# Two-level products in the second half of unit 7, with GpSimd making their sums

## The chip, the cores and the metric

The kernel runs on one core of one Trainium2 chip. Its engines work through queues of their own: TensorE (PE; PEld are its weight loads), VectorE (DVE), ScalarE (ACT), GpSimd (POOL) and SyncE (SP), which issues nearly all DMAs. The metric is the device time of one execution in microseconds; a kernel is given by the median of its runs.

## The reference

A pooled attention is followed by a two-layer network with a snake activation. All of it is f32.

```python
def _attn_ref(q, k, v):                      # (8, 8, 576, 64) each
    k_p = k.reshape(B, H, Sp, pool, D).mean(axis=3)     # pool = 8
    v_p = v.reshape(B, H, Sp, pool, D).mean(axis=3)
    scores = scale * np.matmul(q, k_p.transpose(0, 1, 3, 2))
    scores = scores - np.max(scores, axis=-1, keepdims=True)
    attn = np.exp(scores)
    attn = attn / (np.sum(attn, axis=-1, keepdims=True) + 1e-09)
    return np.matmul(attn, v_p)

def _moe_ref(x, w_in, w_out, alpha):         # x: 4608 x 512, w_in: 512 x 2048
    h = x @ w_in
    s = np.sin(alpha * h)
    g = h + s * s / (alpha + 1e-09)
    return g @ w_out                         # w_out: 2048 x 512
```

The attention's output, its heads side by side, is x.

## The kernel before

**Stages.** The 4608 tokens are cut into nine units of 512 (u = 0 to 8), and the 2048 hidden columns into four groups (J = 0 to 3, n = 4u + J). While the first layer runs for unit u, the attention of batch u + 1 is computed beside it, so that x of unit u + 1 is ready in time; units 7 and 8 have no attention beside them. The activated values g go through HBM (`g_bridge`, method `store_g`, action `st`), and from about 509 us on the second layer runs (`outputs`, line 1309), which reads them back.

**A group.** Its matrix product is done by a Strassen-Winograd scheme: seven products p = 1 to 7 of sums of blocks. The sums of w_in's blocks are made once (tiles a.. and as..), those of x for every unit: `sums_of_x` (line 985; items sx0 to sx3, and sn0 to sn3 for units 1 and 8) writes four blocks into the tile `bt`. A product has four matmuls, M*p*.0 to M*p*.3, each of 128 weights columns by 256 moving columns (`product` in `group`, line 1031). The partial results lie in four PSUM banks, b1, b6, b5, b7, and are carried from bank to bank by copies: c16, c67 (ACT, line 1002), p5 to an SBUF tile. Then a00, a01, a11 add on DVE (line 1001), s.. are sines and q.. squares on ACT (lines 1108 and 1115), f10 adds on DVE and f1 on POOL (line 1060), and st stores the h tile, in two DMAs, one for each half. The h tiles have two buffers, so a group's first write (a00 or a later addition) comes after the store of the group two before it.

**Two-level products.** Some products are themselves done by seven smaller ones of 128 x 128 x 128 (`inner_products`, line 1117; the table `INNER`, line 41): in units 1 to 6, p = 1 in every group and p = 5 in groups 0, 2 and 3, and in group 2 (`INNER_J`) also p = 6 and 7. The steps are i.a, i.b, i.d, i.e1, i.e5 on PE (j.a and so on for the pair 6, 7), each matmul 128 columns wide (line 1130). Between them ACT copies partial results inside PSUM (ca, line 1143; cb, line 1150) and to a small tile (cm, line 1147), and DVE adds (ad, line 1153). The operands of the small products need sums of their own: those of w_in are made once in unit 0 (`inner_w_in`, `inner_w_more`), those of x in every unit by POOL (`inner_x`, `inner_y`, line 983). A group with the pair 6, 7 is begun with a copy of b1 to the tile `seed` (c1); its p5, c16 and c67 are additions on DVE, it has an addition a10 on DVE, and its f10 is on POOL.

**Order.** Every step is an item with a key: 28 to a unit, 7 to a group, plus the number in the table `ORDER`. `perform` (line 1098) issues the items in order of their keys, and this alone sets the order in every engine's queue. The table has a row for the attention's items of a middle unit (`U`), and one for each kind of group (`kind`, line 1087): `first0` to `first3`, `enter`, `mid0` to `mid3`, `exit` (the last group of unit 6), and `end0` to `end3` for both units 7 and 8. `U7` holds sn0 to sn3 and `R` the second layer's preparation: from unit 7 on `load_w_out` (line 837) copies w_out's blocks into place on ACT (line 861) and makes their sums on DVE (line 870), in the steps w0 to w10, and `inner_w` (line 883) follows in v1 to v5, with the tiles we1 and we2 for p = 1 and 2.

**Room.** x of unit u lies in the tile `home` u mod 3; home 0 held unit 6 and isn't used after it. The pool `wo`, with we1 and we2, is opened when unit 7 begins.

```python
        two = self.two(u)
        G.l2 = tuple(p for p in INNER if two and J in INNER[p] and n > self.NJ)
        ...
        G.more = (6, 7) if two and J in INNER_J else ()
        ...
    def two(self, u):
        return 0 < u < self.B - 1
```

Of the kernel before, what the change touches and what calls it, by code (L numbers as in the profile page):

```python
# [13 lines left out]
F32 = mybir.dt.float32  # L14
# [27 lines left out]
INNER_J = (2,)  # L42
ORDER = {
# [5 lines left out]
    "pool_vm": 14.29103999, "pool_v": 15.39643495, "pool_k1": 19.10087875, "clean": 19.11669555, "move": 19.31117787, "values": 24.09941715,  # L49
    "out4": 24.12754471, "qb": 24.20188937, "qc": 24.32802831, "qa": 24.3322157, "out0": 24.34194636, "out2": 24.34888708, "out3": 24.38197436,  # L50
    "k_t": 24.38256879, "sx0": 24.38397247, "qd": 24.39556784, "k_c": 24.4069381, "inner_x": 24.72116763, "out1": 25.02433978, "mark": 25.50536264,
    "sx1": 25.50540264, "qe": 25.61120273, "sx2": 25.78068113, "sx3": 31.53281643},
# [147 lines left out]
class Kernel:  # L200
# [752 lines left out]
    def inner_y(self):  # L953
# [10 lines left out]
        self.sums([(t4[k], R(1, 0)[:, k], t2[:, k], OP.subtract) for k in range(2)])  # L964
        for k, p in enumerate((6, 7)):
            self.X2[p] = {1: R(0, 0)[:, k], 2: R(1, 0)[:, k], 3: R(1, 1)[:, k], 4: t4[k], 5: t1[k], 6: t2[:, k], 7: t3[:, k]}

    def inner_x(self, u):

        steps = []  # L970
# [666 lines left out]
```

## Time and profile before

| | us |
|---|---|
| median of 3 runs (901.91 to 905.1) | 901.98 |
| the profiled execution | 900.14 |
| its span, first to last instruction | 898.4 |
| PE busy | 890.7 |
| DVE busy | 654.3 |
| ACT busy | 456.4 |
| POOL busy | 313.6 |

The profiled execution's own time is 1.7 us above its span and 1.84 us below the median. In the rows quoted below, times are microseconds from the span's start. A row of the timeline gives start, length, engine, line, operation, written and read tiles, the shape, how many instructions were merged, and in brackets the idle time before and what ended it. A row of groups gives the count, the busy time, the mean in nanoseconds and the idle time before. A row of waits gives who waited for whom, the sum, how often, and the longest. An f32 matmul stands in the trace as two records.

### The profile page before, as it was taken

The page shows a single profiled execution, that of the slowest core. Times are in us where ns is not written, and L with a number is a line of the kernel's source. Part 1 is how long each engine was busy: PE and PEld are TensorE (multiplying, and loading weights), DVE is VectorE, ACT ScalarE, POOL GpSimd, SP SyncE. Part 2 cuts the span into 40 slices and gives each one's busy share as a digit, 9 for nine tenths or more (in the row PEclk, how much of TensorE's full clock was granted, in tenths as well). Part 3 has the DMA queues.
Part 4 walks back from the last instruction along what each step waited for, and adds up shares of the span by engine and source line. Part 5 has one row for each costly group of instructions (what it writes and reads, how often), then busy time and mean ns, then how long its engine had stood idle before and what let it go on. Part 6 is the DMA issues. An engine that isn't in the chain of part 4 may idle for free.

```text
span 898.4 us, 18664 instructions
## 1 busy us (share of the span) xinstructions
PE 890.7 (99%) x7218; PEld 816.5 (91%) x7218; DVE 654.3 (73%) x1004; ACT 456.4 (51%) x1079; POOL 313.6 (35%) x327
## 2 busy tenths in 40 slices
PE   8999999999999999999999999999999999999997
PEld 5887888979889898888888999999999999999997
DVE  7575767667566675754346999979798888889894
ACT  5686877878877887877876611111111111121111
POOL 4899967666677766462221200000000000000000
PEclk9999999999999999999999999999999999999999
DMA  9966858667695765557226346251618172534401
GB/s 254 225 199 159 250 173 235 163 187 191 190 266 142 206 196 150 159 161 272 93 101 209 131 129 185 80 182 41 215 39 226 28 220 46 173 92 142 123 14 41
DMA packets 128753, 141.19 MB, mean 157 GB/s; under 512 B 46920, under 2 KB 95704, under 8 KB 128664
## 3 DMA queue, kind: packets, MB, share of 16 engines
q1 hardware_dynamic: 125880, 137.88, 52.9%
q10 hardware_dynamic: 2784, 2.11, 0.9%
q8 instruction: 57, 0.93, 0.4%
q14 instruction: 32, 0.26, 0.1%
HBM read 75.37 MB, written 47.19 MB: 136 GB/s over the span
## 4 chain that ended last, share of the span: by engine, by line
PE 98%; DMA 0%; DVE 0%; ACT 0%; issue 0%; ACTq 0%; DVEq 0%
PE PS L1359 43%; PE PS L1031 39%; PE PS L1130 9%; PE PS L464 2%; PE PS L761 2%; PE PS L774 1%; DMA q<-in_q_dram 0%; PE PS L575 0%; PE PS L554 0%; PE PS L1195 0%; PE PS L421 0%; PE PS L435 0%; PE PS L719 0%; PE PS L362 0%; PE PS L717 0%; PE PS L629 0%
## 5 line engine op out<-in xcount | busy, mean ns | idle before, releaser
L1031 PE MATMUL PS<-home,a 128*128 128x256 f32 x920 | 234.6, 381 | 0.0
L1031 PEld LDWEIGHTS PS<-home,a 128*128 128x128 f32 x920 | 169.6, 190 | 25.6 <-issue 4.7
L1031 PE MATMUL PS<-home,as 128*128 128x256 f32 x680 | 182.3, 382 | 0.0
L1031 PEld LDWEIGHTS PS<-home,as 128*128 128x128 f32 x680 | 123.5, 190 | 14.9 <-POOL as L833 0.2
L1409 POOL TENSOR_TENSOR cc<-cc,cb 128x576 f32<-128x576 f32 x1 | 2.0, 1982 | 373.5 <-DVE cb L1314 373.5
L1060 POOL TENSOR_TENSOR h<-h,s 128x1024 f32<-128x1024 f32 x36 | 86.0, 2390 | 111.6 <-ACT s L1115 109.0
L1359 PE MATMUL PS<-s,wb 128*128 128x144 f32 x896 | 119.1, 286 | 0.0
L1359 PEld LDWEIGHTS PS<-s,wb 128*128 128x128 f32 x896 | 113.6, 190 | 0.0
L1115 ACT ACTIVATE s<-s,c 128x256 f32<-128x256 f32 (+1 forms) x216 | 112.6, 580 | 0.0
L1495 ACT COPY PS<-PS 128x144 f32<-128x144 f32 x56 | 14.7, 263 | 144.1 <-PE PS L1359 138.6
L1108 ACT ACTIVATE s<-h,al 128x256 f32<-128x256 f32 x156 | 69.9, 503 | 21.0 <-DVE h L1001 11.4
L1001 DVE TENSOR_TENSOR h<-PS,s 128x512 f32<-128x512 f32 x66 | 44.4, 684 | 47.3 <-ACT s L1115 35.3
L1359 PE MATMUL PS<-r,wb 128*128 128x144 f32 x512 | 73.3, 286 | 0.0
L1359 PE MATMUL PS<-s,a 128*128 128x144 f32 x512 | 73.2, 286 | 0.0
L1001 DVE TENSOR_TENSOR h<-PS,p 128x512 f32<-128x512 f32 x72 | 48.9, 686 | 27.4 <-PE PS L1031 20.5
L1359 PEld LDWEIGHTS PS<-r,wb 128*128 128x128 f32 x512 | 67.1, 190 | 0.1
L1359 PEld LDWEIGHTS PS<-s,a 128*128 128x128 f32 x512 | 67.0, 190 | 0.0
L290 POOL TENSOR_TENSOR kvin<-kvin 96x768 f32<-96x768 f32 (+3 forms) x42 | 65.0, 1548 | 4.9 <-DMA a<-in_moe_w_in_dram 1.6
L1108 ACT ACTIVATE s<-PS,al 128x256 f32<-128x256 f32 x132 | 55.5, 475 | 10.3 <-PE PS L1031 9.5
L1477 ACT COPY PS<-PS 128x144 f32<-128x144 f32 x56 | 14.7, 263 | 88.3 <-PE PS L1359 88.3
L1359 PE MATMUL PS<-x,wb 128*128 128x144 f32 x384 | 54.9, 286 | 0.0
L1359 PE MATMUL PS<-s,we 128*128 128x144 f32 x384 | 54.7, 286 | 0.0
(239 smaller groups left out, 1609.3 us busy)
## 6 DMA issues: line engine op xcount, KB each, us to landing
g_bridge<-h SPq DMA_DIRECT2D x72, 512.0 KB
r<-g_bridge SPq DMA_DIRECT2D x31, 1152.0 KB
out_dram<-o SPq DMA_DIRECT2D x122, 72.0 KB
kvin<-in_k_dram SPq DMA_DIRECT2D x14, 576.0 KB
q<-in_q_dram SPq DMA_DIRECT2D x7, 1024.0 KB
kvin<-in_v_dram SPq DMA_DIRECT2D x14, 512.0 KB
ex<-tr SPq DMA_DIRECT2D x54, 92.0 KB
ex<-tr SPq DMA_DIRECT2D x54, 88.0 KB
```

The costliest lines, as they stand in the source:

```text
L290: self.nc.gpsimd.tensor_tensor(out=t[..., 0:w] if w > D else out, in0=t[..., 0:w], in1=t[..., w:2 * w], op=OP.add)
L464: nc.tensor.matmul(ps[e][r0 + r:r0 + r + q.shape[-1], h, :], q[s], kb[s, hp, :], start=(e, r0 + r) not in begun, stop=True, skip_group_che ...
L761: nc.tensor.matmul(o[r:r + 64], w, x, start=start and i < 2, stop=False, skip_group_check=True)
L1001: add = lambda o, x, y: nc.vector.tensor_tensor(out=o, in0=x, in1=y, op=OP.add)
L1031: nc.tensor.matmul(ps[:, jj, :], self.A[p][:, kk, f * P:(f + 1) * P], x[:, kk, :], start=start and p not in G.begun, stop=(kk == 1), skip_ ...
L1060: "f1": lambda: nc.gpsimd.tensor_tensor(out=g()[:, :, :, 1], in0=g()[:, :, :, 1], in1=G.s()[:, :, :, 1], op=OP.add),
L1108: self.nc.scalar.activation(out=G.s()[:, i, jj, j, :], in_=src[:, jj], func=AF.Sin, scale=self.al[:, f:f + 1])
L1115: self.nc.scalar.activation(out=x, in_=x, func=AF.Square, scale=self.c[:, f:f + 1])
L1130: nc.tensor.matmul(out, W[m][:, G.J - (INNER_J[0] if p > 5 else 0)], self.X2[p][m], start=start, stop=True, skip_group_check=True)
L1359: nc.tensor.matmul(out, W[:, J // 2, J % 2, :], A[:, J, :], start=(start and J == 0), stop=(J == self.NJ - 1), skip_group_check=True)
L1477: nc.scalar.copy(out=st["x1"][:, 1, :], in_=st["x1"][:, 0, :])
L1495: nc.scalar.copy(out=x1[:, 0, :], in_=x0[:, 1, :])
```

## The change

Unit 7's groups 2 and 3 take two-level products: p = 1, 5, 6, 7 in group 2 and p = 1, 5 in group 3 (`late`, `LATE_J`). Their weights' sums can't be those of unit 0, whose tiles are gone with the attention's pools, so POOL makes them again: `late_w` makes 16 for group 2 and 8 for group 3, in we1 and we2, which lend their room before `inner_w` needs it; the 8 for group 3 overwrite those of p = 1 and 5 of group 2. `late_x` makes the 16 sums of x in home 0. The tiles `seed` and `m5` of unit 7 lie in we2 also. `W2_at` notes from which group on a product's small weights count.

Unit 7's groups 1 to 3 have rows of their own in `ORDER` (`late1` to `late3`), U7 has the new items, and the rows `U`, `end0`, `end1`, `exit`, `mid1` and `mid3` have new numbers; the other rows stay.

```diff
 INNER_J = (2,)
+LATE_J = (2,)
...
 "U7": {
-    "sn0": 27.5, "sn2": 27.50625, "sn1": 27.51, "sn3": 28.24964},
+    "late_x0": 0.9616694, "late_w20": 6.12700667, "late_x1": 6.13293975, "late_w21": 6.13376164, "late_w30": 16.10735295, "sn0": 23.28925745,
+    "sn1": 24.89864805, "sn2": 26.09347972, "sn3": 29.05819944},
...
+    def late_x(self, ps):
+
+        u, bt = self.B - 1, self.bt
+        if 1 in ps:
+            self.room = self.home(0, [P, self.K1, 2 * TH])[:].rearrange("p a b -> p (a b)").rearrange("p (n i m) -> p n i m", i=4, m=P)
+        for p in ps:
+            x = self.xT[u][:, 0:2, 0:TH] if p == 1 else bt[:, p - 5]
+            R = lambda i, j: x[:, i, j * P:(j + 1) * P]
+            t1, t2, t3, t4 = (self.room[:, (1, 5, 6, 7).index(p), i] for i in range(4))
+            self.sums(((t1, R(0, 1), R(0, 0), OP.subtract), (t2, R(1, 1), t1, OP.subtract), (t3, R(1, 1), R(0, 1), OP.subtract), (t4, R(1, 0), t2, OP.subtract)))
+            self.X2[p] = {1: R(0, 0), 2: R(1, 0), 3: R(1, 1), 4: t4, 5: t1, 6: t2, 7: t3}
+
+    def late_w(self, J, ps):
+
+        if J == 2 and 1 in ps:
+            a, b = (self.wo.tile([P, 3, 2, 2, P], F32, name=f"we{i}")[:].rearrange("p a b c d -> p (a b c) d") for i in (1, 2))
+            self.late = [a[:, i:i + 1] for i in range(12)] + [b[:, i:i + 1] for i in range(4)]
+            self.seed = b[:, 4:8].rearrange("p (j i) d -> p j (i d)", j=JW)
+            self.m5 = b[:, 8:10].unsqueeze(2)
+        for p in ps:
+            n = (1, 5, 6, 7).index(p)
+            s1, s2, s3, s4 = self.late[4 * n:4 * n + 4]
+            A = self.A[p][:].rearrange("p k (J j m) -> p k J j m", j=2, m=P)
+            L = lambda i, j: A[:, j, J:J + 1, i]
+            self.sums(((s1, L(1, 0), L(1, 1), OP.add), (s2, s1, L(0, 0), OP.subtract), (s3, L(0, 0), L(1, 0), OP.subtract), (s4, L(0, 1), s2, OP.subtract)))
+            self.W2[p] = {1: L(0, 0), 2: L(0, 1), 3: s4, 4: L(1, 1), 5: s1, 6: s2, 7: s3}
+            self.W2_at[p] = J
...
-        G.l2 = tuple(p for p in INNER if two and J in INNER[p] and n > self.NJ)
+        late = u == self.B - 1 and J > 1
+        G.l2 = tuple(p for p in INNER if late or two and J in INNER[p] and n > self.NJ)
...
-        G.more = (6, 7) if two and J in INNER_J else ()
+        G.more = (6, 7) if late and J in LATE_J or two and J in INNER_J else ()
...
+        if J and u == self.B - 1:
+            return f"late{J}"
...
+        if u == last:
+            for i, ps in enumerate(((1, 5), (6, 7))):
+                at(ORDER["U7"][f"late_x{i}"], self.late_x, ps)
+                for J in LATE_J if i else range(2, self.NJ):
+                    at(ORDER["U7"][f"late_w{J}{i}"], self.late_w, J, ps)
```

Of the new numbers, those that move an item past items of another step (the key is the group's 7n or the unit's 28u plus the number; `mid3` numbers above 7 fall into the next unit):

```diff
 U:    inner_y  8.278 -> 11.712   move 19.311 -> 17.136   sx1 25.505 -> 26.733   sx2 25.781 -> 27.574   inner_x 24.721 -> 25.026
 mid3: q1 12.624 -> 14.114   s01 6.362 -> 14.644   q01 8.176 -> 15.264   f1 16.353 -> 18.660   f10 18.569 -> 18.809   st 18.713 -> 18.943
 exit: f10 10.100 -> 13.134   st 10.168 -> 13.799
```

In a middle unit's keys, f10 of the group before stood at 11.569, ahead of shift3 (11.586), norm0 (11.956) and a01, i.ad and a11 of groups 0 and 1; it now stands at 11.809, behind them and behind norm0 (11.803).

Group 2's steps on PE in unit 7, in the new order, between the last matmul of unit 6 and its own: 38 matmuls of groups 0 and 1, i.a, nine matmuls of group 1, i.b, j.a, i.d, two matmuls, j.b, i.e1, two matmuls, j.d, four matmuls of group 2, j.e6, i.e5, j.e7; then group 3's i.a, three matmuls, i.b.

More of the change, by code (lines that the diff above doesn't have):

```diff
@@ L42 @@
 INNER_J = (2,)
+LATE_J = (2,)
 ORDER = {
 "U": {
[4 rows of a table removed]
[L49 to L52, printed above, removed]
[4 rows of a table added]
+    "pool_vm": 13.97674974, "move": 17.13639355, "pool_v": 18.90634272, "pool_k1": 21.55942806, "clean": 23.9684371, "values": 24.09941715,
+    "qa": 24.23841769, "qc": 24.2794839, "qb": 24.39685794, "out4": 24.42836383, "out0": 25.02338312, "out2": 25.02339305, "out3": 25.02339681,
+    "sx0": 25.02340266, "k_t": 25.02341133, "qd": 25.0263071, "k_c": 25.02636605, "inner_x": 25.02638612, "out1": 25.05042092, "mark": 25.06929668,
+    "qe": 25.5242967, "sx1": 26.73277002, "sx2": 27.57350582, "sx3": 31.42990609},
 "F": {
@@ L938, in inner_w_in @@
         self.W2[p] = {1: L(0, 0), 2: L(0, 1), 3: s4, 4: L(1, 1), 5: s1, 6: s2, 7: s3}
+        self.W2_at[p] = 0
     def inner_w_more(self):
@@ L951, in inner_w_more @@
             self.W2[p] = {1: L(0, 0), 2: L(0, 1), 3: s4, 4: L(1, 1), 5: s1, 6: s2, 7: s3}
+            self.W2_at[p] = n[0]
     def inner_y(self):
@@ L1129, in product @@
             W = self.W2[p]
-            nc.tensor.matmul(out, W[m][:, G.J - (INNER_J[0] if p > 5 else 0)], self.X2[p][m], start=start, stop=True, skip_group_check=True)
+            nc.tensor.matmul(out, W[m][:, G.J - self.W2_at[p]], self.X2[p][m], start=start, stop=True, skip_group_check=True)
         def products(*ms):
@@ L1145, in cm @@
         def cm():
-            m5.append(self.sm.tile([P, 2, 1, P], F32, name="m5", bufs=1)[:, 0:k])
+            m5.append((self.m5 if G.u == self.B - 1 else self.sm.tile([P, 2, 1, P], F32, name="m5", bufs=1))[:, 0:k])
             nc.scalar.copy(out=m5[0], in_=y[:, :, 1:2])
@@ L1564, in run @@
                 self.turn = 4
-                self.W2, self.X2 = {}, {}
+                self.W2, self.X2, self.W2_at = {}, {}, {}
                 self.R = {}
@@ L1575, in run @@
                 att.close()
-                wo = pool(top, "wo", 1, side="right")
+                wo = self.wo = pool(top, "wo", 1, side="right")
                 self.gp = pool(top, "gp", 1, side="right")
```

9 lines of the change are left out of this document (6 added, 3 removed), and 93 rows, old and new, of the table ORDER.

## The prediction

> **What bounds the kernel now.** I read the page first (parts 1, 2 and 4), then the chain of waits in order of time, the stretches by unit, and PE's waits.
>
> ```profile
> span 898.4 us, 18664 instructions
> PE 890.7 (99%) x7218; PEld 816.5 (91%) x7218; DVE 654.3 (73%) x1004; ACT 456.4 (51%) x1079; POOL 313.6 (35%) x327
> PEclk9999999999999999999999999999999999999999
> PE 98%; DMA 0%; DVE 0%; ACT 0%; issue 0%; ACTq 0%; DVEq 0%
> ```
> ```profile
> 407.48 101.64 PE PS L1031 x470
> 509.12 384.31 PE PS L1359 x3136
> ```
> ```profile
> 252.50:307.00 54.50, 54.50 (x487) 47.25 (x490) 36.21 (x64) 43.05 (x98) 36.76 (x42) 1.00 0.70 196
> 407.40:455.00 47.60, 47.60 (x225) 41.91 (x222) 20.38 (x28) 38.01 (x87) 10.17 (x6) 1.00 0.49 177
> ```
> ```profile
> PE PS L1195 <- DVE full L1528: 1.1, 1, 1.1
> ...
> PEld PS L1130 <- DVE PS L1153: 2.3, 6, 0.4
> ```
>
> TensorE is the path: 98% of the chain is PE, its clock is whole, and from 407.48 to the end the chain is two stretches of PE alone. Of the stretches I asked for, 252.5 to 307.0 is one middle unit and 407.4 to 455.0 is about unit 7; in both PE is busy throughout (columns: length, then PE, PEld, DVE, ACT, POOL busy, clock, DMA share, GB/s). PE's longest wait for another engine is 1.1 us, at the start. In the middle only its weight loads are held, 0.4 us at most, once per unit, behind the addition of line 1153. So the time can change in two ways only: by the work that PE is given, and by waits that PE does not have today. In unit 7 POOL is busy 10.17 of 47.60 us, ACT 38.01.
>
> **The change part by part: PE's work.** One product of one level is four matmuls of 256 columns, one of two levels is seven of 128. An f32 matmul leaves two records. Their pace is read from starts:
>
> ```profile
> 411.40 2.75 PE L1031 MATMUL PS<-home,a 128*128 128x256 f32 x12
> 413.99 3.19 PE L1031 MATMUL PS<-home,as 128*128 128x256 f32 x14
> 417.01 2.75 PE L1031 MATMUL PS<-home,a 128*128 128x256 f32 x12
> ```
> ```profile
> 301.96 0.39 PE L1130 MATMUL PS<-last,q 128*128 128x128 f32 x2
> ...
> 302.85 0.60 PE L1031 MATMUL PS<-home,as 128*128 128x256 f32 x2
> ```
>
> (417.01 - 411.40) / 26 = 0.2158 us for a record of 256 columns, and (302.85 - 301.96) / 8 = 0.1113 for one of 128 (four rows of two lie between those starts). A product then goes from 8 x 0.2158 = 1.726 to 14 x 0.1113 = 1.558 us: 0.168 saved. Group 2 of unit 7 changes four products (1, 5, 6, 7), group 3 two (1, 5): 6 x 0.168 = **1.0 us**. That is the whole gain on PE; nothing else leaves its queue.
>
> The Trainium skill, "TensorE: Matmul & The Clock Gate", section "Wait — 56ns, not 53.3ns?", has a warm matmul take its columns at 2.4 GHz and a fixed 2.5 ns; if a record is two passes that would be 215.8 and 109.2 ns, and the six products would save 1.18 us instead. It agrees with the record of 256 columns and is about 2 ns short at 128, so the row decides.
>
> **GpSimd's sums.** Added are 16 sums of x and 24 of weights, all 128x128, on POOL: late_x0, late_w20, late_x1, late_w21 (eight each) stand in POOL's queue behind unit 6's last addition f1 (line 1060), and late_w30 (eight) between the additions of unit 7's groups 0 and 1.
>
> ```profile
> 353.62 0.45 POOL L983 TENSOR_TENSOR ex<-home 128x128 f32<-128x128 f32 x1
> ...
> 355.28 0.45 POOL L983 TENSOR_TENSOR ex<-home 128x128 f32<-128x128 f32 x1
> ...
> 417.53 2.36 POOL L1060 TENSOR_TENSOR h<-h,s 128x1024 f32<-128x1024 f32 x1 [7.06 <-ACT s L1115]
> 432.65 2.37 POOL L1060 TENSOR_TENSOR h<-h,s 128x1024 f32<-128x1024 f32 x1 [12.76 <-ACT s L1115]
> ```
> ```profile
> L983 POOL TENSOR_TENSOR last<-home,last 128x128 f32<-128x128 f32 x12 | 7.7, 641 | 0.0
> ```
>
> Four steps in 1.66 us: 0.415 us a sum. f1 ends at 419.9, the 32 sums at 433.2, just when POOL was idle before (12.76 us until 432.65). When does PE ask? The attention's values move six records ahead, so unit 6's last matmul ends near 407.4 - 1.3 + 36 x 0.2158 = 413.9. By the written order 38 matmuls (76 records, 16.4 us) stand before group 2's i.a, which so starts at 430.3 and first needs sum 13 (425.3). Its j.a comes after i.a, nine matmuls and i.b: 430.3 + 0.89 + 3.88 + 0.89 = 436.0; 0.45 later it needs sum 29, ready at 432.0. Margins 5 and 4.4 us: cost nothing. If that cover is gone, PE waits: at the slow row's 0.641 the 29th is ready at 438.5, 2.1 us late. late_w30 reuses group 2's tiles and must let its i.e5 end, but its first five sums follow earlier readers (i.a, i.b, i.d, i.e1), and between i.e1 and group 3's i.a PE has 4.8 us: nothing. Unit 7's f1 of group 0 queues behind 32 sums, and is due at 432.65 anyway; the store behind it on SP, and group 2's h tile behind that, move by 0.6 us at most. The lent tiles add no wait: home 0 held unit 6's x, read last by M3 before f1 starts, and the first steps of inner_w write we1 and we2 only in unit 8. No DMA is added.
>
> **The copies between the inner steps.** ACT must copy the bank of i.a (i.cm, i.ca) before PE's i.b.
>
> ```profile
> 427.07 2.16 ACT L861 COPY wb<-wb 128x512 f32<-128x512 f32 x4
> ...
> 430.21 0.57 ACT L1002 COPY PS<-PS 128x512 f32<-128x512 f32 x1
> 430.70 0.59 ACT L1002 COPY p<-PS 128x512 f32<-128x512 f32 x1
> 431.17 1.34 ACT L1115 ACTIVATE s<-s,c 128x512 f32<-128x512 f32 x2
> 432.41 0.84 ACT L1108 ACTIVATE s<-PS,al 128x256 f32<-128x256 f32 x2
> 433.12 0.92 ACT L1115 ACTIVATE s<-s,c 128x256 f32<-128x256 f32 x2
> ```
> ```profile
> 271.54 0.58 ACT L1143 COPY PS<-PS 128x512 f32<-128x512 f32 x1
> 272.05 0.90 ACT L1108 ACTIVATE s<-h,al 128x256 f32<-128x256 f32 x2
> 272.86 0.35 ACT L1147 COPY m<-PS 128x256 f32<-128x256 f32 x1
> ```
>
> Group 0's last matmul is the 27th: 413.9 + 11.65 = 425.55. From there ACT has s10 0.84, q1 1.34, a weight copy 1.08, c67 0.57, s00 0.84, q01 0.92, a weight copy 1.08, q00 0.92, p5 0.59, cm 0.35, ca 0.58 = 9.1 us, to 434.7; PE reaches i.b at 430.3 + 0.89 + 3.88 = 435.1. Margin 0.4, gone if the copy ahead of s10 runs late. Group 3's i.b stands only three matmuls (1.29 us) behind its i.a, about as tight. Bounds: 0 to 0.5 at each of the two, so 0 to 1.0 us; I take 0, since row 271.54 is such a copy in the middle units, as tight against PE's row 272.64 below, and PE does not wait there. Of the rest, group 2 turns ACT's copies p5, c16 and c67 into DVE's additions and its f10 into POOL's; over both groups ACT is given three of each of ca, cm, cb and one c1 (4.5 us) for the three copies (1.7), DVE four additions and three ad (4.9 us) for one f10 (0.7). With 38.01 and 20.38 busy of 47.60 us both have room: nothing.
>
> **The new order elsewhere.** In units 1 to 6 and 8 PE's queue changes by swaps of neighbours; sn0 to sn3, which make unit 8's sums on DVE, stay ahead of their readers. In the middle units four moves touch other queues. Additions sx1 and sx2 go behind i.ad and a01 on DVE; inner_x goes behind f1 on POOL, into idle time; inner_y goes behind the previous group's f1, and its consumer j.a comes ten us later; nothing for these. The fourth is f10 of a unit's group 3: on DVE it goes behind a01, i.ad, a11 and norm0. Its store's second half waits for it, on SP with the q and k loads behind; the next group but one reuses the h tile (two buffers), so its a00 waits for that store.
>
> ```profile
> 259.90 1.28 DVE L1001 TENSOR_TENSOR h<-PS,s 128x512 f32<-128x512 f32 x2
> ...
> 265.02 0.69 DVE L1001 TENSOR_TENSOR h<-PS,p 128x512 f32<-128x512 f32 x1 [0.85 <-PE PS L1031]
> 265.63 0.75 DVE L518 TENSOR_REDUCE sm<-ex 128x8 f32<-128x584 f32 x1
> ...
> 270.29 0.69 DVE L1001 TENSOR_TENSOR h<-PS,s 128x512 f32<-128x512 f32 x1 [0.34 <-ACT s L1115]
> ```
> ```profile
> 258.95 2.62 SPq L1163 DMA_DIRECT2D g_bridge<-h  x2
> 261.67 0.42 SPq L243 DMA_DIRECT2D q<-in_q_dram  x1
> ```
> ```profile
> 272.64 0.39 PE L1130 MATMUL PS<-last,q 128*128 128x128 f32 x2
> ```
> ```profile
> g_bridge<-h SPq DMA_DIRECT2D x72, 512.0 KB
> ```
>
> f10 ends at 266.8 instead of 261.2. At the unit's 196 GB/s 512 KB take an estimated 2.7 us alone, 5.4 if the q load behind takes half: landing 269.5 to 272.2. a00 ran at 270.29; ACT's copy (0.58) must end by 272.6, so a00 (0.69) must start by 271.3. The cost is 0 to 0.9 us in each of five units: 0 to 4.5. I take 0, the q load being issued behind the store. A gain is not excluded either: PEld's row of 2.3 us could go, and PE would win that much at the most.
>
> **Sum.** -1.0 + 0 + 0 + 0: span 897.4, the profiled run (900.14, 1.7 us around its span) 899.1. The median of the runs, 901.98, stands 1.84 above that execution; the forecast for it is **901.0 us**.
>
> **Rivals.** One more row is needed, a DVE addition of two SBUF tiles in unit 7:
>
> ```profile
> 418.09 2.35 DVE L991 TENSOR_TENSOR home<-home,home 128x512 f32<-128x512 f32 x1
> ```
>
> (a) ACT's copies are late at both i.b, up to 1.0 us: the gain is eaten, 902.0. For: margins of 0.4. Against: copies as tight hold today.
>
> (b) GpSimd is late. From 0.569 us a sum ((436.4 - 419.9) / 29) PE waits at j.a; at 0.641 it waits 2.1 us: 903.1. For: the 0.641, and the row above, which starts inside POOL's f1 (417.53 to 419.89) and ends 0.55 us behind it, so the two engines hold each other up. Against: 0.415 in the other sums, and one such DVE addition (sx3) between 418 and 433. The Trainium skill, "SBUF — State Buffer", section "SBUF: two separate sides", has a VectorE operation with two SBUF inputs and a GpSimd one exclude each other for a whole instruction; the row agrees.
>
> (c) The other side, slower: the late f10. It decides from a landing behind 271.3; at 272.2 it is 5 x 0.9 - 1.0 = +3.5: 905.5. For: the q load shares the rings. Against: it is issued later, and SP's queue is empty just before.
>
> (d) The new order frees PE of the 2.3 us row: 898.7.
>
> (e) The change does not do what it says: at 0.1233 us a record (1.726 / 14) the seven small matmuls save nothing, 902.0. Against it, the same function runs at 0.1113 in the middle unit.
>
> **How the numbers follow.** Forecast (900.5 to 901.5) 0.50; (a) 0.17; (b) 0.10; (c) 0.14, of which 0.05 beyond 906.5 should norm and moves slip too; (d) 0.06; (e) 0.01; unforeseen 0.02. The range 900.0 to 904.5 holds the forecast, (a), (b) and the lower third of (c), about 0.82. The bound of 0.5% (4.5 us, about what a measurement of this kernel can tell from no change) is wider than the whole gain: faster needs 897.4 and no case gives it, 0.02; slower 0.06; same 0.92.
>
> **What would show it.** Right: L1031 loses 48 records and L1130 gains 84; PE stays busy throughout unit 7, which is 1.0 us shorter; forty more POOL sums near 0.42; no wait of PE for POOL. Wrong: PE or PEld rows waiting for POOL L983 (b), for ACT L1143 near 435 or 447 (a); DVE's a00 idle on a DMA and PE behind it once per unit (c).

## The result, and the profile after

| | before | after |
|---|---|---|
| median of the runs, us | 901.51 (13 runs, 899.66 to 905.1) | 899.72 (13 runs, 897.58 to 901.27) |
| profiled execution, us | 900.14 | 901.0 |
| its span, us | 898.4 | 899.2 |

The ratio is 0.9981, with a 95% interval of 0.9973 to 0.9990: 0.9 to 2.4 us less, 1.7 in the middle. Within half a per cent nothing has changed, as forecast; but 899.72 lies 0.3 us under the range. Two further comparisons of the same kernel gave 0.9985 (0.9976 to 0.9993) and 0.9983 (0.9974 to 0.9992). The profiled execution is one of the longest, so its span tells nothing of the difference. It has to be read stretch by stretch.

The page of the changed kernel, its chain of waits in order of time, and two stretches (one middle unit; unit 7 up to where the traces of both kernels are alike again):

```profile
span 899.2 us, 18818 instructions
PE 891.8 (99%) x7254; PEld 819.5 (91%) x7254; DVE 658.9 (73%) x1010; ACT 458.2 (51%) x1086; POOL 328.9 (37%) x368
PEclk9999999999999999999999999999999999999999
```
```profile
453.09 57.46 PE PS L1088 x266
510.55 384.31 PE PS L1423 x3136
894.89 0.46 DVE cc L1378
895.38 0.51 DVE o L1445
```
```profile
252.50:307.00 54.50, 54.24 (x482) 47.13 (x481) 36.39 (x65) 42.81 (x97) 35.79 (x40) 1.00 0.69 192
408.70:455.00 46.30, 46.30 (x255) 41.32 (x255) 21.62 (x34) 39.39 (x90) 28.00 (x46) 1.00 0.51 182
```

Line numbers have moved: 1031, 1130, 1153 and 1359 of before are 1088, 1189, 1212 and 1423 here. PE has 36 records more (84 of 128 columns for 48 of 256), as the prediction counted. It is busy through all of unit 7, and POOL has gone from 10.17 to 28.00 us there. One thing is new against before: the middle unit has PE idle for 0.26 of 54.50 us. That the chain ends in two instructions of DVE is not new. The view lists only the longest pieces of a chain, and the one that the prediction was read from left them out; asked for its last 20 us, the kernel before has them too:

```profile
893.45 0.47 DVE cc L1314
893.94 0.51 DVE o L1381
```

Behind them come only the last stores of the output: from the end of DVE's last instruction to the end of the span it is 3.9 us before (894.45 to 898.35) and 3.3 after (895.89 to 899.21). So the chain is not PE alone to the end, and this stretch behind PE will matter.

GpSimd's sums on POOL, ACT's copy and PE's step i.b of group 2:

```profile
418.90 2.35 POOL L1117 TENSOR_TENSOR h<-h,s 128x1024 f32<-128x1024 f32 x1 [7.20 <-ACT s L1174]
421.21 0.45 POOL L1039 TENSOR_TENSOR home<-home 128x128 f32<-128x128 f32 x1
...
435.00 0.46 POOL L1039 TENSOR_TENSOR we<-a,we 128x128 f32<-128x128 f32 x1
435.41 2.38 POOL L1117 TENSOR_TENSOR h<-h,s 128x1024 f32<-128x1024 f32 x1
```
```profile
436.59 0.57 ACT L1202 COPY PS<-PS 128x512 f32<-128x512 f32 x1
```
```profile
437.69 0.61 PE L1189 MATMUL PS<-home,we 128*128 128x128 f32 x4
```

The 32 sums take (435.41 - 421.21) / 32 = 0.444 us each, not 0.415; the 29th is ready at 434.1, and j.a, which starts at 438.6 and needs it 0.45 us later, isn't held. ACT's copy ends at 437.16 and PE starts i.b at 437.69: 0.53 us between them, where 0.4 was forecast. At group 3's i.b the copy ends at 448.50 and PE starts at 448.69, 0.19 us behind. So the covers that the prediction named for unit 7 are there, and how thick they are the experiments will show.

PE's and its weight loads' waits have one more line and one longer:

```profile
PE PS L787 <- POOL ex L554: 0.6, 2, 0.4
...
PEld PS L1189 <- DVE PS L1212: 2.7, 7, 0.4
```

The first is new and stands in the middle units: PE waits for a memset of GpSimd's (the item `clean`) ahead of the attention's values (the experiments take it up). The second stood at 2.3, 6 before: the seventh is in unit 7, between i.d and i.e1 of group 3, which have only two matmuls between them:

```profile
450.48 0.61 PE L1189 MATMUL PS<-home,we 128*128 128x128 f32 x4
450.92 1.03 PE L1088 MATMUL PS<-home,a 128*128 128x256 f32 x4
451.93 0.49 PE L1189 MATMUL PS<-home,we 128*128 128x128 f32 x2
452.26 0.39 PE L1189 MATMUL PS<-home,a 128*128 128x128 f32 x2
```
```profile
451.18 0.70 DVE L1212 TENSOR_TENSOR PS<-PS,we 128x512 f32<-128x512 f32 x1 [0.24 <-PE PS L1189]
```

DVE's ad ends at 451.88 and i.e1 starts at 451.93. By the paces of the prediction the four records ahead of it take 0.86 and took 1.01, and its first two take 0.22 and took 0.33: 0.25 us lost. By the starts of single records group 3 loses a little more, 0.05 us in the four records of 256 columns behind i.e1 and 0.02 at its i.b. Where nothing holds them, the 84 small records of unit 7 stand 0.1115 us apart.

**Three stretches.** The records of PE give three marks: the first matmul of the first layer's main part, the first of the last attention's values, and the first of the second layer. What lies ahead of the first mark varied from 21.3 to 23.5 us from one execution to the next, of either kernel, and is left out. The table has the three stretches between the marks and the end for every profiled execution of the study, one to a row; what was changed in each is told below.

| execution | main part to last values | last values to second layer | second layer to end |
|---|---|---|---|
| before | 382.29 | 104.96 | 389.40 |
| null_before | 382.28 | 104.96 | 389.54 |
| before_sp6 | 382.42 | 104.96 | 389.38 |
| before_drain6 | 382.70 | 104.96 | 388.76 |
| before_c67 | 382.19 | 104.96 | 389.35 |
| late_only | 382.22 | 104.31 | 389.34 |
| late_sp6 | 382.29 | 104.35 | 389.43 |
| late_drain6 | 382.25 | 104.32 | 388.76 |
| late_c67 | 383.76 | 104.31 | 388.77 |
| order_only | 381.72 | 106.79 | 388.75 |
| after | 382.09 | 105.17 | 388.82 |
| after_again | 381.80 | 105.17 | 388.75 |
| after_third | 381.61 | 105.16 | 388.78 |
| after_clean | 383.06 | 105.16 | 388.77 |
| act_extra | 381.11 | 107.16 | 388.79 |
| f10_four | 386.60 | 105.16 | 388.76 |
| sums_twice | 380.36 | 123.80 | 388.81 |

The new order puts the last values four records earlier (the prediction had six), so 0.86 us (4 x 0.2158) passes from the first column to the second. With that put back, unit 7 is 104.96 + 0.86 - 105.17 = 0.65 us shorter, the middle units stand between 0.7 longer and 1.1 shorter, and the end is 0.6 us shorter. The 0.65 can be added up: the products give 48 x 0.2158 - 84 x 0.1115 = 0.99 us, as forecast, and group 3 loses 0.32 of it.

### The profile page after: what moved, and what is told of

It reads as the page before. It is cut to its first block, busy times and chain, and to the rows that moved or that the text cites. A ratio compares the mean times of both kernels' runs of the same rounds, so it can differ in the third digit from the quotient of the medians.

```text
span 899.2 us, 18818 instructions
## 1 busy us (share of the span) xinstructions
PE 891.8 (99%) x7254; PEld 819.5 (91%) x7254; DVE 658.9 (73%) x1010; ACT 458.2 (51%) x1086; POOL 328.9 (37%) x368
## 4 chain that ended last, share of the span: by engine, by line
PE 79%; DVE 0%; issue 0%
PE PS L1423 43%; PE PS L1088 25%; PE PS L1189 7%; PE PS L787 1%; PE PS L490 1%; PE PS L800 1%; PE PS L447 0%; DVE o L1445 0%; DVE cc L1378 0%
## 5 line engine op out<-in xcount | busy, mean ns | idle before, releaser
L1088 PE MATMUL PS<-home,a 128*128 128x256 f32 x896 | 232.1, 381 | 0.0
L1088 PEld LDWEIGHTS PS<-home,a 128*128 128x128 f32 x896 | 163.5, 190 | 24.3 <-issue 4.7
L1088 PE MATMUL PS<-home,as 128*128 128x256 f32 x656 | 179.2, 382 | 0.0
L1088 PEld LDWEIGHTS PS<-home,as 128*128 128x128 f32 x656 | 118.9, 190 | 14.0
```

Source lines behind the costliest of these rows:

```text
L1088: nc.tensor.matmul(ps[:, jj, :], self.A[p][:, kk, f * P:(f + 1) * P], x[:, kk, :], start=start and p not in G.begun, stop=(kk == 1), skip_ ...
```

## The experiments

Theory A is the prediction's own: unit 7's products give the gain, the new order gives nothing. B: the order of units 1 to 6 gives something too. C: it costs something.

### How much a comparison is worth

> The kernel before, run against itself, to see what a comparison of this kernel is worth. All theories: ratio 1.000; the half-width of the interval and the spread of single runs (1.3 us either way were seen) say how much of a difference of 1 us can be told.

Every ratio below is against runs of the kernel before made beside it, with its 95% interval in brackets; it is close to the quotient of the two medians, and not quite that. Differences in us are worked out from it. Measured: 1.0002 (0.9994 to 1.0011), 901.46 against 901.48 us, single runs from 899.4 to 902.6. A comparison of 11 or 12 runs tells 0.8 us from nothing. The stretches are far steadier: five traces with the old unit 7 have the last values to the second layer at 104.96 us, every one.

> The changed kernel a second time. Theory A (the forecast's sum, only unit 7 pays): about -1.0 us against before, and the -1.8 first measured was 0.8 us of scatter. Theory B (the new order of units 1 to 6 gives something too): about -1.8 again. Both: PE's new waits behind POOL's memset at the start of the attention's values (0.86 us in unit 1, 0.76 in unit 2, 0.26 in unit 3, 0.14 in unit 4 of the first profiled run) are there again if they belong to the order, and gone if they were a matter of one run.

Measured: 0.9985, so -1.35 us (-2.2 to -0.6). PE waits behind the memset again, but less (0.2 us, and by the starts 0.07 and 0.28 us in units 1 and 2, where the first trace has 0.43 and 0.30 by the same count). They come and go with the execution.

### The order alone and the products alone

```diff
 order_only: before.py with
-the rows U, exit, mid1, mid3 of ORDER as they were
+the same rows as in the changed kernel
 late_only: the changed kernel with
-the rows U, exit, mid1, mid3 of the changed kernel
+the same rows as in before.py
```

> The kernel before with the new numbers of the rows U, exit, mid1 and mid3 alone: unit 7 keeps its one-level products and its rows. Theory A: 0.0 us. Theory B: about -0.8 us. Theory C (what the one trace of the changed kernel shows between the marks of the units: the middle units are longer by the waits behind the memset): +1.1 us. PE's stretch from the first main matmul to the start of the last values is 382.3 us before (21.71 to 403.99) and 382.1 in the changed kernel (23.13 to 405.22): A expects 382.2, B 381.5, C 383.4.

> The changed kernel with the rows U, exit, mid1 and mid3 as they were before: unit 7's two-level products, GpSimd's sums and the rows end0, end1 and late1 to late3 alone. Theory A: -1.0 us. Theory B: -1.0 us, the rest being in order_only. Theory C: -1.8 to -2.9 us, the products being worth more than 6 x 0.168 and the order taking a part back. By the traces: from the start of the last values to the second layer 105.1 us before (403.99 to 509.12), 105.2 less 0.0 in the changed kernel only because its values are issued elsewhere; here A and B expect 104.1, C 103.3 or less.

Measured: order_only 1.0008 (1.0000 to 1.0017), +0.7 us; late_only 0.9995 (0.9986 to 1.0003), -0.45 us. In order_only the first group of unit 7 starts its product 1 in a PSUM bank (M1.2, 3.48 in the keys of unit 6's last group) ahead of that group's a00 (now 4.02), so that by the keys the bank is written over before it is read, and some values of that group are others; the work is the same. Without the new row end0 the new rows don't fit unit 7: there PE loses about 1.0 us more (106.79 against 104.96 + 0.86). late_only shows the products by themselves: main part to second layer 486.53 us against 487.25, 0.7 less, and not 1.0; the 0.25 us at i.e1 of group 3 is in this trace too. What neither theory had is the last column: both kernels with the old rows end in 389.3 to 389.5 us, both with the new rows in 388.8, though the second layer is the same in all.

### The end: a packet of instructions

PE's stretch of the second layer is 384.31 or 384.32 us in all traces; what follows PE's last matmul is 4.9 us before and 4.3 in the changed kernel. The DMA queues in the last 4 us of the kernel before (packets, MB, share of 16 engines) have one packet that isn't a store:

```profile
q10 hardware_dynamic: 626, 0.14, 17.2%
q1 hardware_dynamic: 527, 0.12, 14.7%
q14 instruction: 1, 0.01, 0.5%
```

Theory D: it is SP's next block of instructions, moved when SP comes near the end of the one before, and its place depends on how many instructions SP has; the new rows give SP six more, all of them waits for semaphores (738 for 732).

```diff
     def store_g(self, Q):
         t0 = Q.u * 2 * TH
+        if 8 <= 4 * Q.u + Q.J < 14:
+            self.nc.sync.nop()            # before_sp6, late_sp6
+            self.nc.sync.drain()          # before_drain6, late_drain6, in its place
```

> The kernel before with six no-operations on SP (one ahead of each store of the groups 8 to 13), so that SP's queue has 738 instructions as in the changed kernel, and not 732. In the traces with 732 (the kernel before twice, late_only) an 8 KB packet of the instruction queue is moved 2.8 to 3.0 us before the end, among the last stores of the output; in those with 738 (the changed kernel twice, order_only) the last such packet is 9.9 us or more before the end, and the stretch from the first matmul of the second layer to the end is 388.8 us and not 389.4. Theory D (the packet lengthens the last stores, and its place is a matter of SP's count of instructions): that stretch is 388.8, and the time -0.6 us against before. Rival (the end differs for another reason, the count is chance): 389.4, and 0.0.

> late_only with the same six no-operations on SP: unit 7's two-level products in the old order, and the shorter end. Theory D: 486.5 us from the first main matmul to the second layer as in late_only (before 487.25), 388.8 from there to the end (late_only 389.3); -0.7 - 0.6 = -1.3 us against before. Rival (the end isn't SP's count): -0.7. If the new order of units 1 to 6 is worth nothing on PE, this is at or under the changed kernel.

These two tell nothing of D: the no-operations are not in the program that ran, SP has 732 instructions in both traces, and the end is 389.4 as before. They are repeats of before (1.0001, 0.9992 to 1.0009) and of late_only (0.9993, 0.9983 to 1.0003; 486.64 us to the second layer).

> The kernel before with six drains on SP (0.01 us each at the end of the traces), one ahead of each store of the groups 8 to 13, so that SP has 738 instructions instead of 732 (in before_sp6 the compiler had left the six no-operations out: its trace has 732). Theory D (the 8 KB packet of SP's instruction queue falls among the last stores with 732 and ahead of them with 738, and costs them 0.6 us): first matmul of the second layer to the end 388.8 us (389.34 to 389.54 in five traces with 732), last such packet about 9.9 us before the end, time -0.6 us. Rival (the new order itself shortens the end): 389.4, 0.0.

> Unit 7's two-level products in the old order of units 1 to 6, with the six drains on SP. Theory D and the sum for unit 7 together: 486.6 us from the first main matmul to the second layer (late_only 486.53, late_sp6 486.64, before 487.25), 388.8 from there to the end, so -0.7 - 0.6 = -1.3 us against before, at or under the changed kernel (-0.6 and -0.9 by the stretches of its two traces). Rival of D: -0.7.

Measured: both ends are 388.76 us. The queues in the last 4 us of before_drain6, and its chain's last stretch of PE:

```profile
q10 hardware_dynamic: 660, 0.15, 18.1%
q1 hardware_dynamic: 640, 0.15, 17.6%
```
```profile
510.97 384.32 PE PS L1361 x3136
```

The instruction packet is gone from among the stores (it was moved 10.1 us before the end), and with it 0.6 us, in the old order and without one instruction of the new. All seventeen traces divide in this way: the six with 732 instructions on SP have the packet 2.8 to 3.1 us before the end and a last stretch of 389.3 to 389.5 us; the eleven with 738 have it 9.9 to 10.2 us before, and 388.8. So the end belongs to SP's count, and not to what the change is about. In times: before_drain6 0.9996 (0.9987 to 1.0005), -0.4 us, where the expected -0.6 can't be told from nothing; late_drain6 0.9988 (0.9979 to 0.9997), -1.1 us where -1.3 was expected.

### The new order in the middle units

> The changed kernel with one number changed: the memset (clean) stands at 21.5, ahead of pool_k1 on GpSimd, instead of 23.97, behind it. Theory E (PE's waits behind the memset at the values of units 1 and 2 come from its place behind pool_k1, and are what the new order costs): no wait of PE for the memset; first main matmul to second layer 486.6 us, against 487.26 and 486.97 in the two traces of the changed kernel; -0.35 to -0.65 us against it, so about -1.2 to -1.5 against before by the traces' stretches. Rival (PE waits there for something else that is as late, the k_t transposes or the second memset's order): the waits move to another line, 487.0, 0.0 against the changed kernel.

```diff
-    "clean": 23.9684371,
+    "clean": 21.5,
```

Measured: 1.0001 (0.9987 to 1.0015); main part to second layer 488.2 us, longer than in any trace of the changed kernel. Theory E falls: with the memset out of the way PE still waits at the values of unit 2 (0.2 us, and 0.2 inside them), and 0.9 us at those of unit 3, put down to ACT. What is late is told by another engine's row. DVE's first transposition behind the attention's moves (SP's 16 DMAs from `tr` to `ex`) waits for moves to land, here in unit 1 of the changed kernel:

```profile
130.96 1.25 DVE L402 STREAM_TRANSPOSE tr<-q 128x1024 f32<-128x1024 f32 x1 [1.38 <-DMA ex<-tr]
```
```profile
118.52 11.52 SPq L698 DMA_DIRECT2D ex<-tr  x16
```

and in sums_twice, which has the same instructions up to unit 6:

```profile
130.20 1.25 DVE L402 STREAM_TRANSPOSE tr<-q 128x1024 f32<-128x1024 f32 x1 [0.84 <-DMA ex<-tr]
```
```profile
118.30 10.98 SPq L698 DMA_DIRECT2D ex<-tr  x16
```

The 16 issues begin 0.22 us apart in the two traces and end 0.76 apart. In both a 16 KB packet of instructions falls among the moves; the queues of 2 us around it (from 121.5 in the changed kernel, from 121.3 in sums_twice):

```profile
q8 instruction: 1, 0.02, 4.8%
```
```profile
q8 instruction: 1, 0.02, 3.4%
```

4.8% of 16 engines' 2 us is 1.5 us for that packet, 3.4% is 1.1. The 0.4 us between them is most of the 0.54 by which the issues spread. It falls there in the kernel before as well (1.0 us). But there the moves begin earlier. They go out as soon as DVE's last transposition of the exponentials (the item turn3) is done; its rows before and after, and SP's row before:

```profile
116.53 0.27 DVE L662 STREAM_TRANSPOSE tr<-ex 128x32 f32<-128x32 f32 x2
```
```profile
118.32 0.26 DVE L688 STREAM_TRANSPOSE tr<-ex 128x32 f32<-128x32 f32 x2
```
```profile
116.73 10.81 SPq L672 DMA_DIRECT2D ex<-tr  x16
```

The last values started at 80.46 and 81.82. From there the moves begin 36.27 us later before the change and 36.70 after it, since turn3 is 0.4 us later on DVE, and the last one lands 48.60 and 49.73 us later: 1.1 us more, 0.4 of it from turn3 and the rest from the longer jam. Before, it lands 1.06 us ahead of the next values (130.12); after, 0.35 ahead of them (131.90), and they are what it holds.

So PE's new wait, put down to the memset that ended just ahead, is the landing of the last move. The other traces bear it out. Where PE waits in unit 1 of the changed kernel (after, after_third, act_extra), the last landing is 0.35 us ahead of PE's start; in unit 2 it is 0.24 us ahead in all six traces in which PE waits there. The memset's end is 0.09 to 0.46 us ahead in the same places, and 3.57 in after_clean. In after_third the landing comes behind the memset, and there the list of waits names it:

```profile
PE PS L787 <- DMA ex<-tr: 0.5, 1, 0.5
```

In the nine traces with the old rows the last move lands 0.5 to 1.2 us ahead of the values in unit 1 and 0.65 to 1.4 in unit 2, and PE waits in none. turn3 is 0.48 us later in unit 2. From unit 3 on the moves land 0.5 to 1.2 us ahead in the three traces of the changed kernel, and no start of the values is held.

> The changed kernel a third time, for its middle units: from the first main matmul to the last values 382.09, 381.80, 380.36 (sums_twice) and 381.11 (act_extra) us in four traces of that order up to unit 6, 382.22 to 382.70 in seven of the old one, of which 0.86 is four records that the new order has behind the values instead. Theory F (the new order is worth nothing on the whole in units 1 to 6, and swings by 1.7 us with the landing of the attention's last move, of which 16 KB packets of PE's instruction queue take the rings): between 380.3 and 382.2 again, PE's waits at the values of units 1 and 2 as long as the landing is late; -1.4 us against before (products -0.7, end -0.6, order -0.1). If the order gives a steady gain, 380.4 and -2.4; if a steady loss, 382.1 and -0.6.

Measured: 0.9983 (-1.5 us), main part to last values 381.61. With after, after_again, sums_twice and act_extra that makes five traces of the new order, at 381.4 us in the mean (order_only, at 381.7, is not counted); the seven of the old order ahead of it in the expectation have 382.35. Of the 0.96 between them 0.86 is the four records: the new order gives 0.1 us on the whole, from 1.1 gained to 0.6 lost.

What it can gain is in the values themselves: before the change PE's weight loads there wait for ACT's copy `order`, 1.9 us in five units (1 to 5; the expectation below counts them as 2 to 6):

```profile
PEld PS L761 <- ACT order L768: 1.9, 5, 0.4
```

```diff
 mid3, before.py (before_c67) and late_drain6 (late_c67):
-    "c67": 2.64068989,
+    "c67": 3.12,
```

> The kernel before with one number changed: ACT's copy c67 of a middle unit's last group stands behind the attention's values (3.12 instead of 2.64). In the old order PE's stretch of the values is 3.58 us in the five units 2 to 6 and 3.42 in the others, and in sums_twice, with the new order and no late move, 3.43 to 3.53: ACT's copy 'order', for which the values' last part waits, is 1.70 us behind their start, there 1.26. Theory G (that is what the new order could take from PE in units 1 to 6: it has c67 behind the values too): 3.43 us in each of the five units, -0.8 us in all. Rival (the copy isn't what they wait for): 3.58 and 0.0; or the later c67 holds PE at product 7, above 0.0.

> late_drain6 (unit 7's products, the old order of units 1 to 6, six drains on SP) with that c67 too: -0.7 from the products, -0.6 from the end, -0.8 from c67 if theory G holds: 485.8 us from the first main matmul to the second layer, 388.8 behind it, -2.1 us against before and 0.5 under the changed kernel. If G falls, -1.3.

Measured: before_c67 0.9990 (0.9981 to 0.9999), -0.9 us; late_c67 0.9974 (0.9965 to 0.9984), -2.3 us, median 899.48. The values' stretch (from their start to the next product) is 3.42 to 3.48 us in every unit of both traces, and the wait for `order` is gone from the list: that copy starts 186.56 - 185.30 = 1.26 us behind the values' start in before_c67, 186.13 - 184.43 = 1.70 before:

```profile
186.13 0.14 ACT L768 COPY order<-PS 128x1 f32<-128x1 f32 x1
```
```profile
186.56 0.16 ACT L768 COPY order<-PS 128x1 f32<-128x1 f32 x1
```

The stretches of these two traces don't show the whole 0.8 us, since each has single waits in it (0.69 us within the scores in one, 0.35 at an inner product in the other; in late_c67 also 1.4 us in unit 0, where POOL's sums of w_in were late). late_c67 has the lowest median of the study and stands below before by more than its interval; below the changed kernel by 0.1 to 0.6 us of the three medians, which these runs can't tell.

Gain and loss can now be weighed at the values alone, by the starts, over units 1 to 5. The old order loses 0.8 us there in each of its traces (the two with the later c67 lose nothing); the five of the new order lose 0.2 to 1.3 us, 0.9 in the mean. So the new order takes away one wait, brings another of about that size, and is worth nothing on the whole.

### The rivals' thresholds

```diff
 f10_four:   f10 on DVE, last group of units 1 to 5: done four times
 sums_twice: each step of late_x and late_w done twice
 act_extra:  cm of the pair 1, 5 in unit 7 done four times
```

> The changed kernel with DVE's f10 of the last group done four times over in the units 1 to 5 (same result each time): it ends 3 x 0.69 = 2.07 us later, so that the store's second half lands at 274.8 instead of 272.7 in the unit whose a00 starts at 273.75 and must start by 274.0 for PE's i.b at 275.36. Rival (c) of the prediction has its threshold there: a00 is late by about 0.8 us and PE by as much, once in each of five units: +4.0 us against the changed kernel (2.7 to 5). If the store's landing doesn't hold a00, 0.0.

Measured: 1.0049 (1.0029 to 1.0069), +4.4 us against before. Main part to second layer is 4.5 to 5.0 us above the three traces of the changed kernel. PE's waits, and a00 on DVE:

```profile
PE PS L1189 <- ACT PS L1202: 3.7, 5, 0.9
```
```profile
269.90 2.81 DVE L1058 TENSOR_TENSOR h<-PS,s 128x512 f32<-128x512 f32 x4
...
276.06 0.69 DVE L1058 TENSOR_TENSOR h<-PS,s 128x512 f32<-128x512 f32 x1 [2.44 <-DMA g_bridge<-h]
```

Five waits, 0.74 us in the mean, where 0.8 was expected: the chain f10, store, a00, ACT's copy, PE of rival (c) is as the prediction drew it, and the change stops a little over 1 us short of it (2.07 us of delay cost 0.74).

> The changed kernel with unit 7's two cm copies of the pair 1, 5 done four times over (3 x 0.33 = 1.0 us more on ACT ahead of ca, once in group 2 and once in group 3). Rival (a) of the prediction, with its margins as the trace of the changed kernel has them: ca ends at 437.16 for PE's i.b at 437.69 (0.53 free), and at 448.50 for 448.69 (0.19 free). So PE waits 0.5 us in group 2 and 0.8 in group 3: +1.3 us from the last values to the second layer (105.17 to 106.5), and as much in the time. If ACT's copies had room, 0.0.

Measured: 1.0007 (0.9996 to 1.0017), about 2 us above the changed kernel; last values to second layer 107.16, 2.0 above. PE's two waits:

```profile
435.66 0.68 PE L1189 MATMUL PS<-home,we 128*128 128x128 f32 x4 [0.58 <-ACT PS L1202]
447.85 0.68 PE L1189 MATMUL PS<-home,we 128*128 128x128 f32 x4 [0.96 <-ACT PS L1202]
```

0.58 and 0.96 for the expected 0.5 and 0.8. These are counted from the modelled end of a matmul; by the starts the two holds are 0.82 and 1.19 us and make up the whole 2.0. ACT's copies end at 435.51 and 447.70, so a held PE starts 0.15 us behind the copy. With that taken off, the changed kernel has 0.38 us of room in group 2 (0.53 - 0.15), as rival (a) had it, and 0.04 in group 3 (0.19 - 0.15), which it called about as tight: there the change stands at the limit.

> The changed kernel with each of GpSimd's 40 late sums done twice. Rival (b) of the prediction: GpSimd is on no path at 0.42 to 0.445 us a sum and decides from 0.569. By its account: the sums begin at 421.2; group 2's i.a needs the 26th at 432.9 and has it at 432.8, no wait; j.a needs the 58th at 439.0 and has it at 421.2 + 58 x 0.445 = 447.0: PE waits 8.0 us there, then up to 2 us more for the doubled late_w30 at group 3's i.a. Against the changed kernel +8 to +10 us. If GpSimd's sums had room to spare beyond what I think, 0 to 2.

Measured: 1.0194 (1.0177 to 1.0210), +17.5 us; last values to second layer 18.6 us above the changed kernel, twice what was expected. PE's waits in order, then ACT's longest:

```profile
432.02 0.71 PE L1189 MATMUL PS<-home,we 128*128 128x128 f32 x4 [0.45 <-POOL we L1039]
443.72 0.80 PE L1189 MATMUL PS<-home,we 128*128 128x128 f32 x2 [5.77 <-POOL we L1039]
447.61 1.65 PE L1189 MATMUL PS<-home,we 128*128 128x128 f32 x6 [3.09 <-POOL we L1039]
455.18 1.22 PE L1189 MATMUL PS<-home,we 128*128 128x128 f32 x4 [4.21 <-ACT PS L1202]
```
```profile
453.74 0.91 ACT L1167 ACTIVATE s<-h,al 128x256 f32<-128x256 f32 x2 [15.78 <-POOL h L1117]
```

PE waits 9.3 us for the sums themselves, within the expected 8 to 10. The 4.21 us are a chain that the prediction had not followed: f1 of group 0 stands on POOL behind the sums, ACT's next sine waits for f1 (its 15.78 us), and ACT's copy for PE stands behind the sine. By the starts the four holds are 14.4 us; the other 4.2 of the 18.6 are the clock (below).

## Why the prediction was wrong

**No measurable change by the half per cent, as forecast, and a gain, as forecast; its size was wrong.** Forecast: 901.0 us, 1.0 below before, in a range from 900.0. Measured: 899.72, and 1.35 to 1.7 below before.

**The step that failed** is the sentence that the time can change in two ways only, by PE's work and by PE's waits, which was drawn from a chain read as PE alone to the end. The chain goes on for some 5 us behind PE's last matmul, and there the new order takes 0.6 us off: a term that the sum does not have. Two terms of the sum failed beside it. PE's work was put at -1.0 and measured -0.65, and the median that the forecast was taken from was 0.5 us high. The parts in turn:

**Its base.** The forecast was taken from the median of three runs, 901.98. Thirteen runs have 901.51, and later ones 901.29 to 901.52: the base was 0.5 us high. That is 0.5 of the 1.3 us between forecast and result, and the range had nothing for it, though the three runs already lay 3.2 us apart.

**PE's work, -1.0:** mechanism right, term too large. The records are as counted, but unit 7 is 0.6 to 0.7 us shorter (late_only, late_sp6, late_drain6 and three traces of the changed kernel), for the 0.32 us that group 3 loses, 0.25 of it in the wait at i.e1. The prediction had quoted that wait's row, PEld 2.3 us in six places, and took it only for a possible gain in the middle units; it is what a group with the pair 1, 5 in this order costs, and group 3 brought a seventh.

**GpSimd's sums, 0:** right, with 0.444 us a sum and 4.9 us to spare at j.a for the forecast 4.4. The sentence that f1 of group 0 "is due at 432.65 anyway" was right in that f1's place costs nothing here, and no bound: doubled sums make ACT wait for it, and PE for ACT.

**ACT's copies, 0:** right; 0.38 us of room in group 2 for the forecast 0.4, and in group 3 next to none, where luck had a part.

**The new order elsewhere, 0 to +4.5, taken as 0:** right as a mean (-0.1 us), and for f10 right in its chain too (f10_four). What failed is that all other moves of the order were costed at nothing. The prediction followed each changed item to the next reader, but not the attention's chain norm, turn3, the 16 moves on SP, values; it named "norm and moves" only as a remote addition to (c). turn3 is 0.4 us later on DVE, the margin of 0.5 to 1.2 us before the values is used up when a packet of instructions holds the moves for long, and PE loses 0.2 to 1.3 us at the values in a trace. The other way, c67 behind the values takes a wait of 0.16 us from PE in each of five units. The prediction did not look for it: it lies in the rows of the weight loads only. That the two come to nothing together is luck, and not what the 0 stood for.

**The end, not in the sum: -0.6.** The prediction notes that no DMA is added, and says nothing of the stores behind PE. The new rows give SP six instructions more, and an instruction packet that had fallen among the last stores no longer does.

Together: -0.7 from unit 7, -0.1 from the order, -0.6 from the end, -1.4 us; the runs have -1.35, -1.5 and -1.7. The three profiled executions of the changed kernel by themselves have -0.6, -1.0 and -1.2 between the first mark and the end (against 876.73 us, the mean of before, null_before and before_sp6), -0.9 in the mean, a smaller gain than the middle of any of the three intervals and at the edge of the first. Whether that is the scatter of three executions or something in the start is open: the first mark stands at 22.9 us in the mean of the nine traces with the old rows and at 22.3 in the eight with the new, but single traces of either lie up to 2 us apart.

Rival (d), a gain beyond the forecast, was the side on which the result came out, but not its mechanism: the waits of the 2.3 us row are all still there, and there is one more. (a), (b), (c) and (e) did not happen.

## What to carry to other kernels

When a forecast is a microsecond in nine hundred, the base needs as many runs as the result, and stretches between marks on the bounding engine tell more than the times: here one trace showed 0.65 us in unit 7 where twelve runs could not. A changed order is to be followed on every in-order queue to its last item, SP's with its stores and moves too, since a move goes out only when the engine that writes its source is done. A chain of waits is to be read to its last piece: what lies behind the bounding engine's last instruction is time as well. A waiting row names the last releaser only: when its engine was done in good time, look for a DMA.

## What the runs showed of the hardware

**Instructions come by DMA, in among the data.** Over all traces an 8 KB packet took 0.3 to 0.9 us and a 16 KB packet 0.9 to 2.0 us, 0.9 to 1.6 among the moves of units 1 and 2. In unit 1 of the changed kernel, with such a packet under way from 121.80 to 123.34, a move issued at 120.61 had fifteen of its sixteen parts landed by 122.70 and the last at 124.44: one part in sixteen was late, and the move with it. Among the last stores a packet of 8 KB costs 0.6 us of the kernel's time. Six instructions more on SP take that away; in before_drain6 these were drains of 0.12 to 0.51 us each, some 660 us or more ahead of the end.

**PE's clock after a wait.** In sums_twice the stretches of time (columns as before; the clock is the third from the right) and two rows of PE show what a wait of some microseconds costs beside itself:

```profile
437.00:444.00 7.00, 1.23 (x10) 1.04 (x9) 1.01 (x2) 0.36 (x1) 6.29 (x15) 0.90 0.00 1
444.00:450.00 6.00, 2.91 (x11) 2.43 (x12) 0.65 (x2) 0.00 (x0) 5.43 (x13) 0.50 0.00 0
450.00:455.00 5.00, 0.97 (x3) 0.25 (x1) 4.97 (x5) 1.26 (x3) 4.86 (x4) 0.50 0.08 29
455.00:460.00 5.00, 4.82 (x19) 4.46 (x20) 0.11 (x1) 3.12 (x9) 4.21 (x10) 0.53 0.49 181
460.00:466.00 6.00, 6.00 (x43) 5.53 (x42) 3.88 (x6) 5.27 (x12) 4.71 (x7) 1.00 0.00 0
```
```profile
456.19 0.63 PE L1189 MATMUL PS<-home,as 128*128 128x128 f32 x2
...
462.06 0.39 PE L1189 MATMUL PS<-home,as 128*128 128x128 f32 x2
```

PE's pause of 5.77 us begins at about 437.95. The mean clock of 0.90 up to 444 puts the fall to one half at about 442.6, 4.7 us into the pause; that of 0.53 from 455 to 460 puts the return to full at about 459.7, 4.5 us after PE is busy again at 455.18. At half clock two records of 128 columns are 0.43 us apart from the two behind them, by the starts, and 0.22 at full clock (the rows' own lengths, 0.63 and 0.39, run to a modelled end). The Trainium skill, "TensorE: Matmul & The Clock Gate", section "What's actually happening", has the clock halved after one idle window of about 3.4 us and whole again after one busy window; the trace agrees, with these 4.7 and 4.5 us. So a price for a long wait on PE has a second part: here some 4 of the 18.6 us (8.7 us of PE's busy time ran at half clock).
